# Attention and a cosine MLP in one hand-planned kernel: other landing times for loads and other costs for small operations in its planner, and the first product's scale made per chunk

## The chip, the cores and the metric

The kernel runs on one core of a Trainium2 chip. Its engines are TensorE (PE, matrix products, with its weight loads shown as PEld), VectorE (DVE), ScalarE (ACT), GpSimd (POOL) and SyncE (SP, which issues DMAs). The metric is the time of one execution on the device in microseconds.

## The reference, cut to what matters

The inputs are q, k and v of shape 8 x 8 x 576 x 64 (batch, heads, positions, width), a weight matrix w_in of 512 x 2048 and a matrix w_out of 2048 x 512.

```python
# attention, once on positions averaged in fours, once on a local band
q_d, k_d, v_d = (a.reshape(B, H, S // 4, 4, D).mean(axis=3) for a in (q, k, v))
out_up = np.repeat(sm_attn(q_d, k_d, v_d), 4, axis=2)
mask = np.abs(pos[:, None] - pos[None, :]) < 4
out_local = softmax(where(mask, scale * q @ k.T, -1e9)) @ v
x = (out_up + out_local).transpose(0, 2, 1, 3).reshape(4608, 512)
# the MLP
h = x @ w_in                      # 4608 x 2048
return (h * np.cos(h)) @ w_out    # 4608 x 512
```

## The kernel before, in words

**Two halves.** The attention half works through 8 batches of 4 pairs of heads, 32 units in all. A unit loads q and k (`u_qk`) and a layout of v (`u_v`), forms the scores on PE (`u_s`), transposes (`u_t`) and multiplies with v (`u_pv`), which writes a part of x. `v_sum` adds up v in fours for batches 2 to 7, by one plain load and three DMAs of POOL that add to it.

The MLP half works on tiles of 384 tokens, 12 in all, and on 16 chunks of 128 columns of w_in. `gemm1` makes h for one tile and one chunk (12 products, line 982). `cosine` turns it into g: ACT rounds the scaled h to an integer (L1054), DVE takes the difference (L1055), ACT takes the sine (L1057), DVE multiplies by h and a factor rho (L1058), and the result is stored as two half-precision parts, gh (L1060 on ACT or L1061 on DVE) and gl (L404, on POOL or DVE). `gemm2` multiplies gh and gl by the rows of w_out (9 products, L1079). From tile 5 on, pairs of chunks are made with fewer products (`gemm1_pair`, L1021).

The first three tiles go through blocks of chunks, because the weights arrive during that time: chunk 0, chunk 1, chunks 2 to 4 (2 and 3), then 0 to 4 for the other two tiles, and 4 to 8, 8 to 12 and 12 to 16 for all three. Later tiles take all 16 chunks in one block.

**Weights and scales.** `w_load` loads a chunk of w_in or w_out as 64-bit numbers (512 KB, L427). `w_split` turns them into two half-precision parts: ACT takes an absolute value (L439), DVE does four steps (L440 to L446), ACT squares and sums (L452), PE totals, and DVE reads an exponent (L465). From it small operations make the scale wsc (L468), wexp (L470) and wsum (L471), and with wsc the two parts are made (L477 to L480). For x, `v_norm` loads v once more in four pieces a batch (288 KB each) and squares them on ACT (L499); `x_scale` turns that into a scale for a group of two batches. Three kinds of scale per block follow: `g_scale` gives rho (L562, L564) for a whole block, `h_scale` gives hs, the scale in L1054 and L1055 (L572, L574), and the output's scale os (L577 to L581).

**What sets the order.** Nothing in the kernel is ordered by hand, except PE's MLP products and the chains of loads. Each operation is entered with an engine, a cost in us (`dur`), a time `lat` that must pass after its end before what depends on it may start, and perhaps a second engine as an alternative. `Plan.run` places the operations forward, each on the engine that comes free, by a priority that a backward pass over the same costs has set. Of eight such rounds the shortest is taken, and its order on every engine is the program. At run time each engine issues in that order, and semaphores make it wait for data; an operation whose data is late holds up what stands behind it.

The cost of a load is its size by 262 KB a us, at least 0.45, and it lands `lat` later:

```python
def dma(nbytes, fn, r=(), w=(), pw=()):
    o = pl.op("SP", max(0.45, nbytes / 262e3), fn, r=r, w=w, pw=pw, lat=1.8)
```

The weight loads form a chain in which each waits in the plan for the one before. Loads of `u_qk`, `u_v`, `v_norm` and `v_sum` for batches 2 to 7 may come after the w_out load of chunk 6. The raw weights have 7 buffers, the pieces of v_norm two, the q and k of later units three each, vl two.

A small operation (`small`) is planned on POOL, with DVE as the alternative at 0.08 us. The planner takes the alternative where it would end earlier by a tolerance of 0.3 us.

Of the kernel before, what the change touches and what calls it, by code (L numbers as in the profile page):

```python
# [16 lines left out]
AF = mybir.ActivationFunctionType  # L17
ALU = mybir.AluOpType
# [16 lines left out]
NF = 4  # L35
# [17 lines left out]
ONE = 2.0 ** 23  # L53
# [4 lines left out]
TS = 5  # L58
# [242 lines left out]
def _act(n, psum=True, extra=0):  # L301
    return n * 0.000833 + (0.051 if psum else 0.093) + 0.093 * extra


def _dve(n):
    return n * 0.001042 + 0.065


def _dvs(n):
    return n * 0.001042 + 0.125  # L310
# [7 lines left out]
def attn_ffn_kernel(ctx: ExitStack, tc: tile.TileContext, qT, kT, vdn, vl, w_in, w_out, out):  # L318
    nc = tc.nc
    pe, act, dve, pool, sp = nc.tensor, nc.scalar, nc.vector, nc.gpsimd, nc.sync  # L320
# [6 lines left out]
    pl = Plan()  # L327

    def sb(tag, n, shape, dtype=F32, name=None, pool=None):
        t = pl.turn(tag, n)  # L330
        return pl.buf(lambda: (pool or ap).tile(shape, dtype, name=name or tag, tag=t, bufs=1), t)
# [9 lines left out]
    bquart, bhalf = const.tile([P, 1], F32, name="bquart"), const.tile([P, 1], F32, name="bhalf")  # L341
# [30 lines left out]
    for t in range(NT):  # L372
        r = (t - TS) % (NX - 1)
# [20 lines left out]
    loads, size = {}, {}  # L394

    def dma(nbytes, fn, r=(), w=(), pw=()):
        o = pl.op("SP", max(0.45, nbytes / 262e3), fn, r=r, w=w, pw=pw, lat=1.8)
        size[o] = nbytes if w else 0
        loads.setdefault((pl.name,) + pl.arg, []).append(o)
        return o  # L400

    def sub(n, out, in0, in1, **kw):

        f = lambda e: lambda: e.tensor_tensor(out=out(), in0=in0(), in1=in1(), op=ALU.subtract)  # L404
        pl.op("POOL", _pool(n), f(pool), alts=[("DVE", _dve(n), f(dve))], **kw)

    def small(e, fn, r=(), w=(), pw=()):
        o = {"POOL": ("DVE", 0.08, lambda: fn(dve)), "DVE": None}[e]
        pl.op(e, 0.16 if e == "POOL" else 0.08, lambda: fn({"POOL": pool, "DVE": dve}[e]), r=r, w=w, pw=pw, alts=[o] if o else [])

    def tile1(tag, shape, dtype=F32):
        return pl.buf(lambda: const.tile(shape, dtype, name=tag, tag=tag, bufs=1), tag)
# [17 lines left out]
    exps = {}  # L430
# [53 lines left out]
    xexp = {g: tile1(f"xe{g}", [P, 1]) for g in range(B // GRP)}  # L484
# [1 line left out]
    vq = {g: tile1(f"vq{g}", [P, 8 if g == 0 else 4 * GRP]) for g in range(B // GRP)}  # L486
    vzero = pl.buf(None)
    pl.op("POOL", 0.1, lambda: pool.memset(vq[0].get(), 0.0), w=[vzero])
    hscale, gscale, oscale, passmax = {}, {}, {}, {}

    def later(name, shape):
        n = 2 if name == "vl" else 3
# [73 lines left out]
    def h_scale(g, c0, c1, v):  # L566
        pl.name = "h_scale"
        s, o = (tile1(f"hs{g}{c0}{c1}{v}", [P, c1 - c0], I32), tile1(f"os{g}{c0}{c1}{v}", [P, 1]))
        we, known = (pairexp.get, [paired]) if v else (lambda: wexp.get()[:, 0], [exps[c] for c in range(c0, c1)])
        d, e1, i1 = sb("hd", 2, [P, NC]), sb("oe", 2, [P, 1]), sb("oi", 2, [P, 1], I32)  # L570
        hscale[(g, c0, c1, v)], oscale[(g, c0, c1, v)] = s, o
        small("POOL", lambda e: e.tensor_scalar(out=d.get()[:, :c1 - c0], in0=we()[:, c0:c1], scalar1=xexp[g].get(), scalar2=-29.0,  # L572
                                                op0=ALU.add, op1=ALU.add), r=known + [xexp[g]], w=[d])
        small("POOL", lambda e: e.tensor_scalar(out=s.get(), in0=d.get()[:, :c1 - c0], scalar1=1.0, scalar2=ONE, op0=ALU.max, op1=ALU.mult),  # L574
              r=[d], w=[s])
        pm = passmax[(c0, c1, v)]
        small("POOL", lambda e: e.tensor_scalar(out=e1.get(), in0=pm.get(), scalar1=xexp[g].get(), scalar2=-96.0 if v else -92.0, op0=ALU.add, op1=ALU.add),  # L577
              r=[pm, xexp[g]], w=[e1])
        small("POOL", lambda e: e.tensor_scalar(out=e1.get(), in0=e1.get(), scalar1=1.0, scalar2=254.0, op0=ALU.max, op1=ALU.min), w=[e1])
        small("POOL", lambda e: e.tensor_scalar(out=i1.get(), in0=e1.get(), scalar1=ONE, scalar2=None, op0=ALU.mult), r=[e1], w=[i1])  # L580
        small("POOL", lambda e: e.tensor_scalar(out=o.get(), in0=i1.get().bitcast(F32), scalar1=-2.0 * PI, scalar2=None, op0=ALU.mult),  # L581
              r=[i1], w=[o])
# [45 lines left out]
    def vsum_of(b):  # L628
        if b not in vsum:
            vsum[b] = sb("vsum", 2, [HD, NPAIR, 2, P])  # L630
        return vsum[b]

    def v_sum(b):
        pl.name = "v_sum"
        t = vsum_of(b)
        dst = lambda: t.get().rearrange("p g a n -> p (g a n)")
        src = lambda r: vdn[b][:, r].rearrange("p g a n -> p (g a n)")
        dma(8 * HD * NPAIR * P, lambda: sp.dma_start(dst(), src(0)), w=[t])
        for r in range(1, 4):
            pl.op("POOL", 1.0, lambda r=r: pool.dma_start(dst(), src(r), accum_op=ALU.add), w=[t], lat=6.0)  # L640

    def u_vd(b, pr):
        pl.name = "u_vd"
# [351 lines left out]
    def gemm1_pair(t, p, c0, c1):  # L995
# [45 lines left out]
        add(2, lambda: h1().rearrange("p (i n) -> p i n", i=2), R1, both("ph.1"), [M4, M5], [L1, R1])  # L1041
        cosine(t, 2 * p, c0, c1, h0, [L0, R0])
        cosine(t, 2 * p + 1, c0, c1, h1, [L1, R1])

    def cosine(t, c, c0, c1, h, own):
        m = SIZE[t]
        tr = sb("tr", 4, [P, m], pool=fp)
        gh, gl = sb("gh", LAG + 2, [P, m], F16, pool=fp), sb("gl", LAG + 2, [P, m], F16, pool=fp)
        ti = lambda: tr.get().bitcast(I32)
        g = t // 3  # L1050
        hs, gs = hscale[(g, c0, c1, t >= TS)], gscale[(c0, c1, t >= TS)]
        inv = lambda: hs.get()[:, c - c0:c - c0 + 1].bitcast(F32)
        rho = lambda: gs.get()[:, c - c0:c - c0 + 1].bitcast(F32)
        pl.op("ACT", _act(m, True, 2), lambda: act.activation(ti(), h(), AF.Identity, bias=bquart, scale=inv()), r=own + [hs], w=[tr])  # L1054
        pl.op("DVE", _dvs(m), lambda: dve.scalar_tensor_tensor(out=tr.get(), in0=h(), scalar=inv(), in1=ti(),  # L1055
                                                               op0=ALU.mult, op1=ALU.subtract), r=own + [hs], w=[tr])
        pl.op("ACT", _act(m, False, 1), lambda: act.activation(tr.get(), tr.get(), AF.Sin, scale=2.0 * PI, bias=bhalf), w=[tr], tab="sin")  # L1057
        pl.op("DVE", _dvs(m), lambda: dve.scalar_tensor_tensor(out=tr.get(), in0=tr.get(), scalar=rho(), in1=h(),  # L1058
                                                               op0=ALU.mult, op1=ALU.mult), r=own + [gs], w=[tr])
        pl.op("ACT", _act(m, False), lambda: act.activation(gh.get(), tr.get(), AF.Copy), r=[tr], w=[gh],  # L1060
              alts=[("DVE", _dve(m / 2), lambda: dve.tensor_copy(gh.get(), tr.get()))])  # L1061
        sub(m, gl.get, tr.get, gh.get, r=[tr, gh], w=[gl])
        gt[(t, c)] = (gh, gl)
# [65 lines left out]
    for c in range(NC):  # L1129
        for k, d in (("i", 0.0), ("o", 0.2)):  # L1130
            t = need[c - c % NF] + 0.4 * (c % NF) if c >= NF else need[c]
# [21 lines left out]
    for b in range(2, B):  # L1153
        t0, t1 = tile_of(b * S), tile_of(b * S + S - 1)
        lo, hi = (done[t1 - NX + (t1 >= TS + NX - 1)] if t1 >= NX else 20), first[t0]
        for i in range(NPAIR):

            last = max(lo - 2.5 + (hi - lo - 1.0) * i / (NPAIR - 1), last + 1.5)
            if b % GRP == 0 and i == 0:
                for j in range(GRP):  # L1160
                    at(last - 6.0 + j, v_norm, b + j)
                at(last - 3.5, x_scale, b // GRP)
            if i == 0:
                at(last - 3.0, v_sum, b)
            unit(last, 1.4, 2.5, b, (0, 2, 1, 3)[i])
    for i in range(len(steps) + LAG):
        if i < len(steps):
            t, c, c0, c1 = steps[i]
# [6 lines left out]
    for t, i, f, a in sorted(ev, key=lambda e: e[:2]):  # L1175
        pl.now, pl.arg = t, a
        pl.boost = BOOST.get(a[0], 0.0) if f in (u_qk, u_v, u_vd, u_s, u_t, u_pv, x_scale, v_sum) else 0.0
        if f is u_vd or f is w_split and a[1] == 0 or f is g_scale and a[1] <= NF or f is h_scale and a[2] <= NF:
            pl.boost = BOOST[0]
        f(*a)  # L1180
# [24 lines left out]
    def spare(t0, t1):  # L1205
        best = None
        for own in spans.values():
            for x, y in zip(own, own[1:] + [[1e9]]):
                if x[1] < t1 <= y[0] + 1e-6:
                    if best is None or (max(x[1], t0), x[1]) < best[:2]:  # L1210
                        best = (max(x[1], t0), x[1], x[2])
        return best
# [3 lines left out]
    with tc.manual_schedule():  # L1216
        constants()
        for o in order:
            if o.eng == "PE" and o.start < CFG["fend"]:

                ahead = o.name in ("u_s", "u_t", "u_pv") and o.arg[0] == 0
                s = (last, 0.0, idle) if ahead else spare(last, o.start)
                early = o.name in ("u_s", "u_t", "u_pv") and o.arg[0] < NEARLY
                n = min(int((o.start - s[0] - CFG["fgap"]) / (0.23 if last < 5 else CFG["fstep"])), 16) if s else 0
# [47 lines left out]
```

## Time and profile before

| | |
|---|---|
| median of 3 runs | 995.46 us |
| lowest, highest | 988.75 us, 1001.65 us |
| the profiled execution | 998.38 us, span 996.6 us |
| PE busy | 936.8 us, 94% of the span |
| DVE busy | 808.0 us, 81% |
| ACT busy | 623.4 us, 63% |
| POOL busy | 271.4 us, 27% |
| DMA moved | 84.95 MB, mean 85 GB/s |

The span is the time from the first to the last recorded instruction. Times inside it count from its start. A wait is idle time of an engine put down to what ended it. "DMA to landing" is the time from a DMA's issue until its data is there. The granted clock of TensorE is given as a share of full speed.

### The profile page before, as it was taken

Reading aid. Unit: us, or ns where it says so; the run is one execution under the profiler, and the core shown is the slowest. Engines: PE = TensorE matmul, PEld = TensorE weight load, DVE = VectorE, ACT = ScalarE, POOL = GpSimd, SP = SyncE. Lnnn points to the kernel's source line nnn. Section 1 sums busy time; section 2 is a strip of 40 time slices with the busy share of each in tenths; the row PEclk is TensorE's granted clock in tenths of the full one; section 3 lists DMA queues with packets and bytes.
Section 4 is the critical chain, followed back from the end, with each engine's and each line's share of the span. In section 5 each row is a group of like instructions: output and inputs, shape, how many; then the busy total and the mean of one; then the engine's idle time right before and its main releaser. Section 6 shows DMA issues by size and latency. Waiting matters only on the chain.

```text
span 996.6 us, 28859 instructions
## 1 busy us (share of the span) xinstructions
PE 936.8 (94%) x12163; PEld 612.4 (61%) x12163; DVE 808.0 (81%) x1701; ACT 623.4 (63%) x1342; POOL 271.4 (27%) x401
## 2 busy tenths in 40 slices
PE   5799778989999999999999999999999999999998
PEld 3666334544555555555567666766777677676765
DVE  5889758688897876789997999897779988877775
ACT  2546757887676765656665665765567666655554
POOL 3534744242252230134431143140021311200000
PEclk8989799999999999999999999999999999999999
DMA  8643697873334451140020241140022110000000
GB/s 239 203 169 92 187 241 224 230 197 69 52 82 114 109 117 42 49 113 25 2 73 18 65 123 42 43 120 2 17 74 66 42 50 18 2 33 2 33 1 32
DMA packets 42729, 84.95 MB, mean 85 GB/s; under 512 B 4136, under 2 KB 14632, under 8 KB 42600
## 3 DMA queue, kind: packets, MB, share of 16 engines
q1 hardware_dynamic: 36120, 69.15, 21.6%
q0 software_dynamic: 6480, 13.96, 9.2%
q8 instruction: 95, 1.56, 0.7%
q14 instruction: 34, 0.28, 0.1%
HBM read 65.01 MB, written 18.09 MB: 83 GB/s over the span
## 4 chain that ended last, share of the span: by engine, by line
PE 50%; DVE 21%; ACT 6%; DMA 3%; issue 3%; POOL 1%; POOLq 0%; DVEq 0%; SPq 0%; ACTq 0%
PE bank L1079 22%; PE bank L1021 15%; PE bank L982 6%; DVE tr L1058 3%; DVE tr L1055 3%; PE bank L942 2%; DVE room L1027 2%; PE bank L703 2%; DVE gl L404 2%; DMA k<-kT 2%; DMA norm<-vdn 1%; ACT tr L1054 1%; DVE room L404 1%; PE bank L930 1%; ACT tr L1057 1%
## 5 line engine op out<-in xcount | busy, mean ns | idle before, releaser
L1079 PE MATMUL bank<-wo,gh 128*128 128x512 f16 x1152 | 346.6, 383 | 8.7 <-ACT gh L1060 4.6
L1079 PE MATMUL bank<-wo,gl 128*128 128x512 f16 x576 | 220.3, 383 | 5.7 <-POOL gl L404 3.7
L1079 PEld LDWEIGHTS <-gh 128*128 128x128 f16 x1152 | 109.0, 99 | 100.3 <-issue 11.3
L1057 ACT ACTIVATE tr<-tr,bhalf 128x384 f32<-128x384 f32 x192 | 117.3, 613 | 52.0 <-DVE tr L1055 50.6
L982 PEld LDWEIGHTS <-wi 128*128 128x128 f16 x960 | 94.4, 99 | 84.0 <-issue 18.5
L1027 DVE TENSOR_TENSOR room<-room,bank 128x384 f32<-128x384 f32 x224 | 111.6, 499 | 40.1 <-PE bank L1021 35.9
L1021 PEld LDWEIGHTS <-wi 128*128 128x128 f16 x1344 | 115.5, 98 | 24.8 <-issue 3.9
L1060 ACT ACTIVATE gh<-tr 128x384 f16<-128x384 f32 x167 | 87.1, 523 | 35.7 <-DVE tr L1058 33.8
L404 DVE TENSOR_TENSOR gl<-tr,gh 128x384 f16<-128x384 f32 x159 | 91.5, 577 | 17.9 <-ACT gh L1060 15.5
L1079 PEld LDWEIGHTS <-gl 128*128 128x128 f16 x576 | 56.7, 98 | 78.0 <-POOL gl L404 5.7
L1021 PEld LDWEIGHTS <-room 128*128 128x128 f16 x1008 | 86.4, 98 | 16.9 <-issue 4.8
L1058 DVE SCALAR_TENSOR_TENSOR tr<-tr,rho016True,room 128x384 f32<-128x384 f32 x112 | 71.3, 640 | 12.9 <-ACT tr L1057 12.5
L982 PE MATMUL bank<-x0h,wi 128*128 128x384 f16 x256 | 70.6, 339 | 10.2 <-DVE tr L1058 10.0
L404 POOL TENSOR_TENSOR gl<-tr,gh 128x384 f16<-128x384 f32 x33 | 35.8, 1085 | 156.4 <-ACT gh L1060 103.9
L1054 ACT ACTIVATE tr<-room,bquart,hs3016True 128x384 int32<-128x384 f32 x48 | 33.9, 707 | 53.5 <-DVE room L1027 53.3
L1054 ACT ACTIVATE tr<-room,bquart,hs2016True 128x384 int32<-128x384 f32 x48 | 33.6, 706 | 42.0 <-DVE room L1027 42.0
L942 PEld LDWEIGHTS bank<-sml,vl 32*64 32x64 f32 x3072 | 49.2, 135 | 8.4 <-issue 6.3
L942 PE MATMUL bank<-sml,vl 32*64 32x24 f32 x3072 | 52.6, 214 | 1.5 <-DVE mxl L728 1.1
L760 POOL TENSOR_TENSOR sml<-sml,su 128x384 f32<-128x384 f32 x19 | 21.6, 1134 | 114.5 <-DVE su L758 114.5
L982 PE MATMUL bank<-x0l,wi 128*128 128x384 f16 x128 | 43.3, 339 | 0.0
L1105 POOL DMA_DIRECT2D out<-ob x33 | 30.4, 1075 | 46.8 <-ACT ob L1096 41.0
L703 PE MATMUL bank<-k,q 64*32 64x32 f32 x3072 | 35.7, 196 | 6.8 <-issue 6.4
(312 smaller groups left out, 2117.8 us busy)
## 6 DMA issues: line engine op xcount, KB each, us to landing
vl<-vl SPq DMA_DIRECT2D x32, 384.0 KB, 3.3
q<-qT SPq DMA_DIRECT2D x32, 292.0 KB, 3.6
k<-kT SPq DMA_DIRECT2D x32, 292.0 KB, 4.6
out<-ob SPq DMA_DIRECT2D x36, 256.0 KB, 2.0
out<-ob POOLq DMA_DIRECT2D x33, 256.0 KB, 5.7
wd<-w_in SPq DMA_DIRECT2D x16, 512.0 KB
wd<-w_out SPq DMA_DIRECT2D x16, 512.0 KB, 5.1
norm<-vdn SPq DMA_DIRECT2D x24, 288.0 KB, 5.5
```

Of the source, the lines that this page charges most:

```text
L404: f = lambda e: lambda: e.tensor_tensor(out=out(), in0=in0(), in1=in1(), op=ALU.subtract)
L703: pe.matmul(to()[BS * w:BS * (w + 1), j - c.start], q.get()[hs, o:o + BS], k_.get()[hs, o:o + BS], start=not early, stop=not early or j == ...
L942: pe.matmul(banks[e].get()[64 * h:64 * h + 64, o:o + BQ], vt.get()[r, a, i, :], sml.get()[r, 4 * a + i, :BQ], start=True, stop=True)
L982: pe.matmul(ph.get()[:, :m], w[:, i, kc, :], x[:, kc, :], start=(n == 0), stop=(n == 3 * KC - 1))
L1021: pe.matmul(to.get(), blk(a)[:, kc], x_parts(t)[b][0 if main else 1][:, i, kc], start=(n == 0), stop=(n == 5))
L1027: pl.op("DVE", _dve(n * HT), lambda: dve.tensor_tensor(out=out(), in0=wide(one.get()), in1=two(), op=ALU.add), r=r, w=w)
L1054: pl.op("ACT", _act(m, True, 2), lambda: act.activation(ti(), h(), AF.Identity, bias=bquart, scale=inv()), r=own + [hs], w=[tr])
L1057: pl.op("ACT", _act(m, False, 1), lambda: act.activation(tr.get(), tr.get(), AF.Sin, scale=2.0 * PI, bias=bhalf), w=[tr], tab="sin")
L1058: pl.op("DVE", _dvs(m), lambda: dve.scalar_tensor_tensor(out=tr.get(), in0=tr.get(), scalar=rho(), in1=h(), op0=ALU.mult, op1=ALU.mult), r ...
L1060: pl.op("ACT", _act(m, False), lambda: act.activation(gh.get(), tr.get(), AF.Copy), r=[tr], w=[gh], alts=[("DVE", _dve(m / 2), lambda: dve ...
L1079: pe.matmul(o, (gh, gh, gl)[k].get()[:, sl], wo.get()[:, (0, 1, 0)[k]], start=(c == c0 and k == 0), stop=(c == c1 - 1 and k == 2))
L1105: pl.op("POOL", 1.0, lambda dst=dst, ob=ob: pool.dma_start(dst, ob.get(), accum_op=ALU.add), r=[ob], w=[part[(t, i)]], lat=6.0)
```

## The change

Three numbers of the planner change, and one scale is made in smaller pieces.

- Loads of batches 2 to 7 land later in the plan: `lat` is 6.0 for v_norm, 7.0 for the plain load of v_sum, 5.0 for u_qk and u_v, in place of 1.8. Weight loads of chunks 4 and up have 4.0. The three adding DMAs of v_sum have 9.0 in place of 6.0.
- A small operation costs 0.35 us on POOL in the plan, in place of 0.16. The alternative on DVE stays at 0.08.
- For blocks of at most four chunks (`NF` is 4), `h_scale` makes hs chunk by chunk, two small operations for each, and L1054 and L1055 depend on the piece of their own chunk. Other blocks are made whole, as before.

The arithmetic stays as it is.

```diff
     def dma(nbytes, fn, r=(), w=(), pw=()):
-        o = pl.op("SP", max(0.45, nbytes / 262e3), fn, r=r, w=w, pw=pw, lat=1.8)
+        far = {"v_norm": 6.0, "v_sum": 7.0, "u_qk": 5.0, "u_v": 5.0}.get(pl.name) if pl.arg and pl.arg[0] not in (0, 1) else None
+        if pl.name == "w_load" and pl.arg[1] >= NF:
+            far = 4.0
+        o = pl.op("SP", max(0.45, nbytes / 262e3), fn, r=r, w=w, pw=pw, lat=far or 1.8)
...
     def small(e, fn, r=(), w=(), pw=()):
-        pl.op(e, 0.16 if e == "POOL" else 0.08, ...)
+        pl.op(e, 0.35 if e == "POOL" else 0.08, ...)
...
     def h_scale(g, c0, c1, v):
-        small("POOL", lambda e: e.tensor_scalar(out=d.get()[:, :c1 - c0], in0=we()[:, c0:c1], ...), r=known + [xexp[g]], w=[d])
-        small("POOL", lambda e: e.tensor_scalar(out=s.get(), in0=d.get()[:, :c1 - c0], ...), r=[d], w=[s])
+        n = c1 - c0 if v or c1 - c0 > NF else 1
+        for c in range(c0, c1, n):
+            e_, z, some = pl.buf(None), slice(c - c0, c - c0 + n), known if v else [exps[k] for k in range(c, c + n)]
+            small("POOL", lambda e, c=c, z=z: e.tensor_scalar(out=d.get()[:, z], in0=we()[:, c:c + n], ...), r=some + [xexp[g]], w=[e_], pw=[d])
+            small("POOL", lambda e, z=z: e.tensor_scalar(out=s.get()[:, z], in0=d.get()[:, z], ...),
+                  r=[e_, d], w=[hparts.setdefault((g, c0, c1, v, c), pl.buf(None))], pw=[s])
+            for k in range(c, c + n):
+                hparts[(g, c0, c1, v, k)] = hparts[(g, c0, c1, v, c)]
...
     def v_sum(b):
-            pl.op("POOL", 1.0, lambda r=r: pool.dma_start(dst(), src(r), accum_op=ALU.add), w=[t], lat=6.0)
+            pl.op("POOL", 1.0, lambda r=r: pool.dma_start(dst(), src(r), accum_op=ALU.add), w=[t], lat=9.0)
...
     def cosine(t, c, c0, c1, h, own):
+        hp = hparts[(g, c0, c1, t >= TS, c)]
-        ... act.activation(ti(), h(), AF.Identity, bias=bquart, scale=inv()), r=own + [hs], w=[tr])
+        ... act.activation(ti(), h(), AF.Identity, bias=bquart, scale=inv()), r=own + [hp], w=[tr])
-        ... op0=ALU.mult, op1=ALU.subtract), r=own + [hs], w=[tr])
+        ... op0=ALU.mult, op1=ALU.subtract), r=own + [hp], w=[tr])
```

More of the change, by code (lines that the diff above doesn't have):

```diff
@@ L408, in small @@
         o = {"POOL": ("DVE", 0.08, lambda: fn(dve)), "DVE": None}[e]
-        pl.op(e, 0.16 if e == "POOL" else 0.08, lambda: fn({"POOL": pool, "DVE": dve}[e]), r=r, w=w, pw=pw, alts=[o] if o else [])
+        pl.op(e, 0.35 if e == "POOL" else 0.08, lambda: fn({"POOL": pool, "DVE": dve}[e]), r=r, w=w, pw=pw, alts=[o] if o else [])
     def tile1(tag, shape, dtype=F32):
@@ L488, in attn_ffn_kernel @@
     pl.op("POOL", 0.1, lambda: pool.memset(vq[0].get(), 0.0), w=[vzero])
-    hscale, gscale, oscale, passmax = {}, {}, {}, {}
+    hscale, gscale, oscale, passmax, hparts = {}, {}, {}, {}, {}
     def later(name, shape):
@@ L571, in h_scale @@
         hscale[(g, c0, c1, v)], oscale[(g, c0, c1, v)] = s, o
[L572 to L575, printed above, removed]
+        n = c1 - c0 if v or c1 - c0 > NF else 1
+        for c in range(c0, c1, n):
+            e_, z, some = pl.buf(None), slice(c - c0, c - c0 + n), known if v else [exps[k] for k in range(c, c + n)]
+            small("POOL", lambda e, c=c, z=z: e.tensor_scalar(out=d.get()[:, z], in0=we()[:, c:c + n], scalar1=xexp[g].get(), scalar2=-29.0,
+                                                              op0=ALU.add, op1=ALU.add), r=some + [xexp[g]], w=[e_], pw=[d])
+            small("POOL", lambda e, z=z: e.tensor_scalar(out=s.get()[:, z], in0=d.get()[:, z], scalar1=1.0, scalar2=ONE, op0=ALU.max, op1=ALU.mult),
+                  r=[e_, d], w=[hparts.setdefault((g, c0, c1, v, c), pl.buf(None))], pw=[s])
+            for k in range(c, c + n):
+                hparts[(g, c0, c1, v, k)] = hparts[(g, c0, c1, v, c)]
         pm = passmax[(c0, c1, v)]
@@ L1051, in cosine @@
         hs, gs = hscale[(g, c0, c1, t >= TS)], gscale[(c0, c1, t >= TS)]
+        hp = hparts[(g, c0, c1, t >= TS, c)]
         inv = lambda: hs.get()[:, c - c0:c - c0 + 1].bitcast(F32)
         rho = lambda: gs.get()[:, c - c0:c - c0 + 1].bitcast(F32)
-        pl.op("ACT", _act(m, True, 2), lambda: act.activation(ti(), h(), AF.Identity, bias=bquart, scale=inv()), r=own + [hs], w=[tr])
+        pl.op("ACT", _act(m, True, 2), lambda: act.activation(ti(), h(), AF.Identity, bias=bquart, scale=inv()), r=own + [hp], w=[tr])
         pl.op("DVE", _dvs(m), lambda: dve.scalar_tensor_tensor(out=tr.get(), in0=h(), scalar=inv(), in1=ti(),
-                                                               op0=ALU.mult, op1=ALU.subtract), r=own + [hs], w=[tr])
+                                                               op0=ALU.mult, op1=ALU.subtract), r=own + [hp], w=[tr])
         pl.op("ACT", _act(m, False, 1), lambda: act.activation(tr.get(), tr.get(), AF.Sin, scale=2.0 * PI, bias=bhalf), w=[tr], tab="sin")
```

## The prediction

> **What bounds the kernel now.** I read the page first for the totals, then the table of stretches for where TensorE (PE) is short of work, then the list of waits inside those stretches, and last the timeline around the longest wait.
>
> ```profile
> span 996.6 us, 28859 instructions
> PE 936.8 (94%) x12163; PEld 612.4 (61%) x12163; DVE 808.0 (81%) x1701; ACT 623.4 (63%) x1342; POOL 271.4 (27%) x401
> 0.00:100.00 100.00, 80.45 (x1942) 58.16 (x1943) 80.03 (x209) 48.50 (x147) 40.22 (x65) 0.90 0.58 176
> 100.00:275.00 175.00, 151.47 (x823) 79.74 (x820) 133.26 (x267) 125.98 (x262) 69.35 (x119) 0.94 0.66 170
> 275.00:400.00 125.00, 120.86 (x1961) 71.88 (x1947) 97.11 (x220) 82.86 (x175) 35.45 (x53) 1.00 0.41 93
> 400.00:950.00 550.00, 541.93 (x7143) 374.25 (x7142) 468.19 (x955) 344.26 (x718) 126.43 (x164) 1.00 0.16 46
> ...
> 125.00:150.00 25.00, 18.28 (x93) 9.15 (x91) 13.64 (x28) 13.03 (x26) 10.89 (x16) 0.93 0.93 241
> 200.00:225.00 25.00, 21.41 (x119) 11.48 (x117) 20.38 (x43) 21.10 (x47) 11.30 (x20) 1.00 0.72 198
> ```
>
> The rows of stretches give the stretch and its length, then the busy us (and instructions) of PE, PE's weight load, VectorE (DVE), ScalarE (ACT) and GpSimd (POOL), the granted clock, the busy share of the DMA engines and GB/s. The kernel is bound by PE: 936.8 of 996.6 us. The stretches say where that is not true. From 400 to 950 us PE lacks 550.00 - 541.93 = 8.1 us, so hardly anything can be won there. From 275 to 400 it lacks 4.1 us. From 100 to 275 us, where the weights are loaded and split and the first products run, it lacks 175.00 - 151.47 = 23.5 us, and the granted clock is 0.94. Before 100 us the two first batches run, whose loads keep their 1.8 us; only the small operations change there. So what the change is worth is decided between 100 and 275 us, and at most some 25 to 30 us lie there. The waits of that stretch:
>
> ```profile
> ACT norm L499 <- DMA norm<-vdn: 12.8, 5, 7.7
> DVE wv L440 <- ACT wv L439: 7.5, 1, 7.5
> ACT wi L477 <- POOL wsc L468: 5.0, 4, 2.2
> PE bank L1079 <- ACT gh L1060: 4.6, 1, 4.6
> PE bank L1079 <- POOL gl L404: 3.7, 3, 2.7
> DVE vm L518 <- ACT norm L499: 3.0, 1, 3.0
> ```
>
> Columns: who waited for whom, total us, times, longest. The first, second and fourth are one event, which the timeline shows (start, duration, engine, line, in brackets the wait before it):
>
> ```profile
> 126.69 0.38 SPq L427 DMA_DIRECT2D wd<-w_in  x1
> ...
> 127.12 1.23 SPq L510 DMA_DIRECT2D norm<-vdn  x2
> ...
> 138.54 0.33 PE L982 MATMUL bank<-x2h,wi 128*128 128x384 f16 x1
> 142.26 0.68 ACT L499 ACTIVATE norm<-norm 128x576 f32<-128x576 f32 x1 [7.69 <-DMA norm<-vdn]
> ...
> 143.50 0.67 PE L1079 MATMUL bank<-wo,gh 128*128 128x512 f16 x2 [4.64 <-ACT gh L1060]
> ...
> 144.04 0.68 DVE L440 TENSOR_SCALAR wv<-wv 128x512 f32<-128x512 f32 x1 [7.51 <-ACT wv L439]
> ```
>
> ACT issues in order. At 134.6 it reached the square of a v_norm piece (L499) whose load had left SP at 127 and landed at 142. Behind it stood the rounding gh (L1060), for which PE waited, and the Abs of the next weights (L439), for which DVE waited. The plan had put the square there because it reckoned that load at 288 KB / 262e3 + 1.8 = 2.9 us.
>
> **The change, part by part.** All terms are set against the profiled execution, 998.4 us (span 996.6 and 1.8 around it). It lies 2.9 us above the median of 995.46, inside the spread of 988.75 to 1001.65.
>
> *1. v_norm reckoned at 6.0 + 1.1 us.* What the loads really took from 100 to 175 us, then all weight loads from 100 to 275, then the page's medians:
>
> ```profile
> DMA to landing us min/median/max: 5.0/10.0/15.1
> DMA to landing us min/median/max: 4.1/5.3/7.3
> k<-kT SPq DMA_DIRECT2D x32, 292.0 KB, 4.6
> norm<-vdn SPq DMA_DIRECT2D x24, 288.0 KB, 5.5
> ```
>
> The new figure of 7.1 us is between the median of the busy stretch (10.0) and that of all (5.5); the old one was under the minimum of 5.0. With it the planner finds gh and Abs ready before the square and puts them ahead. The stall goes from ACT for 7.1 - 2.9 = 4.2 of its 7.7 us at least, and with the work put ahead probably all of it goes from PE. PE gets back its 4.6 us of idling, and the slow restart behind it:
>
> ```profile
> 143.40:147.50 4.10, 3.67 (x9) 0.58 0.84 290
> 239.77 1.94 PE bank L1079 x9
> ```
>
> Nine products took about 4.0 us at a granted clock of 0.58, where nine take 1.94 later: 2 us more. So 6.6 us are in reach for PE and 7.5 for DVE. What is late next is DVE, whose row is dense again from 144 us on, fed by the weight loads. Those weights had been issued by 127 us and land within 4.1 to 7.3 us, so they would be there. I take -5, bounds 0 and -7.5. The other four waits on norm, 5.1 us, by stretch, 175 to 200 and 200 to 225 us:
>
> ```profile
> ACT norm L499 <- DMA norm<-vdn: 2.8, 1, 2.8
> ...
> ACT norm L499 <- DMA norm<-vdn: 2.3, 3, 0.9
> ```
>
> From 200 to 225 PE lacks 25.00 - 21.41 = 3.6 us, in which what both waits hold up would have to come back; I take -2, bounds 0 and -3.6.
>
> [...]
>
> *2. u_qk and u_v at 5.0, v_sum at 7.0 and its sums at 9.0.* From 300 to 400 us:
>
> ```profile
> DVE qkd L622 <- DMA k<-kT: 4.5, 3, 2.3
> DVE qkd L622 <- DMA q<-qT: 3.2, 2, 2.1
> ```
>
> 7.7 us of DVE idling, while PE lacks only 4.1 us in that stage and has products queued. I take -1, bounds 0 and -4. POOL waits for vsum, but PE's waits name POOL only at gl, so I cost that at nothing. POOL's slack hides it (69.35 busy of 175). On SP the longer figures raise these loads against the weight loads behind which they queue; SP issues in order, and each norm load first waits for its buffer (two buffers). What this moves is in the bounds of the next term.
>
> *3. w_load of chunks 4 and up at 4.0.* These loads were not waited for:
>
> ```profile
> L439 ACT ACTIVATE wv<-wd 128x512 f32<-128x512 f32 x16 | 10.1, 668 | 0.1
> ```
>
> 0.1 us of idling before 16 of them. So nothing is won. If the plan now holds each split back by 4.0 - 1.8 = 2.2 us and that falls on the end of a block, the three blocks (4 to 8, 8 to 12, 12 to 16) lose 6.6 us together. I take 0, nearest to the row, bounds 0 and +6.6.
>
> *4. Small operations at 0.35 us, and more of them.* Blocks of at most four chunks, all in the first three tiles, are 1+1+2+4+4+4+4 = 20 chunks in 7 blocks, with two operations each. That is 40 instead of 14, so 26 are added. Rows of those there are now:
>
> ```profile
> L562 POOL TENSOR_SCALAR pd12False<-wsum,pm12False 128x1 f32<-128x1 f32 x1 | 5.6, 5582 | 0.1
> L572 POOL TENSOR_SCALAR hd<-wexp,xe 128x4 f32<-128x4 f32 (+3 forms) x7 | 3.5, 493 | 0.7
> L574 POOL TENSOR_SCALAR hs024False<-hd 128x2 int32<-128x2 f32 x1 | 0.9, 935 | 0.1
> L572 DVE TENSOR_SCALAR hd<-wexp,xe x1: 200/200/200, 59.4 to 59.4; 128x1 f32<-128x1 f32 x1
> ...
> 111.34 0.61 PE L1079 MATMUL bank<-wo,gl 128*128 128x512 f16 x1 [2.67 <-POOL gl L404]
> ```
>
> (The first three rows end in busy us, mean ns and idle before; the fourth gives min/median/max ns.) At the 0.49 of seven such operations 26 are 12.8 us of POOL time; on DVE, at 0.2, 5 us. Eight of them (blocks 2 to 4 and 0 to 4) fall near 100 to 110 us, where POOL's chain of scales stood ahead of gl and PE waited 2.7 us for it. Eight at 0.49 make that 3.9 us longer. With 0.35 the planner sees a longer queue and may give gl to DVE, and the 2.7 us go. I take 0, bounds -2.7 and +3.9. Earlier scales themselves win little: Sin may start earlier, but the next product of rho and h still waits for the whole block's rho, which stays as it was, and with it the two banks. So that half is 0.
>
> *5. The rest is planned anew.* From 400 us on the order shifts by itself: 8.1 us lie there to win, and a plan can lose as much as it wins. I take 0, bounds half of that each way, -4 and +4.
>
> The sum: -5 - 2 - 1 + 0 + 0 + 0 = -8, so 990.4 for an execution like the profiled one and **987.5** at the median.
>
> **The rivals.** *The wait only moves* (994): the DMA engines are 0.93 busy from 125 to 150 us, so the norm data come no sooner and each load of them frees its buffer later. The square is then late for x_scale (DVE vm waited 3.0 us for it), and PE waits elsewhere in the same stretch. For it speaks that DVE has 133 us of work in 175; against it that ACT, which stalled, is busy for only 13.03 of the 25 us. That the change does not do what it says, because SP is held by buffers and not by the plan, comes to the same time. [...]
>
> *Slower, by POOL* (1003): POOL's operations are not 0.35 long but as long as DVE lets them. pd12 on one element took 5.58 us while DVE ran its two-input splits; hs024 took 0.94. If the eight added ones near the first block cost that 0.94, they hold wsc and gl back by 7.5 us; all 26 at 0.49 are 12.8 us and give 1008, and with the 6.6 of term 3 1015. It decides from the point where they stand on POOL ahead of wsc or gl. For it: ACT waited 5.0 us for wsc already. Against it: the longer 0.35 sends them to DVE. [...]
>
> *Much faster* (973): all good ends together, 7.5 + 3.6 + 4 + 2.7 + 4 = 21.8 us below 995.46. For it: a stall ahead of the first blocks delays every stage behind it.
>
> **How the numbers follow.** Forecast 0.43; the wait moves, or the change does nothing, 0.18; shorter landing 0.05; slower by POOL 0.19; much faster 0.15. The likeliest gives 987.5. The range 972 to 1008 runs from the good ends together to the 26 operations at 0.49 us; about 0.08 lies below and 0.11 above. A change under 2% (19.9 us) can hardly be told from none here, as three runs spread over 13 us. Faster than 975.6 is nearly all of the much faster case, 0.14; slower than 1015.4 takes a third of the POOL rival with the weights late on top, 0.07; within is 0.79.
>
> **What would show it.** Right: no wait of ACT on norm over 2 us, PE busy over 21 of 25 us from 125 to 150, a clock of 1.0 there, DVE's waits for q and k below 3 us, and the stages after 400 us as long as now. Wrong: PE waiting for wsc or gl at 100 to 112 us longer than 2.7 us, POOL operations over 1 us there, ACT L439 waiting for its loads or standing idle ahead of a block's end, x_scale late. The number fails if the new plan also changes the first 100 us, which I costed at nothing though PE lacks 19.6 us there.

## The result, and the profile after

The changed kernel takes 987.55 us (median of 20 runs, 981.85 to 993.68) where the kernel before takes 996.98 us beside it (20 runs). The ratio is 0.9915, with a 95% interval of 0.9889 to 0.9941: a gain of 0.6 to 1.1%. Some executions of one kernel lie over 1.5% above its fastest; here and below, medians count them and ratios and intervals leave them out. The profiled execution took 986.07 us. First the span and the busy row of the kernel after, from its page:

```profile
span 984.3 us, 28932 instructions
PE 943.4 (96%) x12172; PEld 619.3 (63%) x12172; DVE 813.0 (83%) x1730; ACT 630.3 (64%) x1350; POOL 267.0 (27%) x390
```

The span is 12.3 us shorter, and PE is busy for 6.6 us more, although its work is nearly the same. So the time was won at idle PE, and some of PE's work ran slower. The table of stretches of the kernel after (columns as in the prediction) says where:

```profile
70.00:80.00 10.00, 8.87 (x237) 6.81 (x236) 8.32 (x25) 5.88 (x24) 1.80 (x2) 0.94 0.02 4
80.00:90.00 10.00, 9.73 (x216) 7.54 (x213) 5.78 (x13) 3.64 (x10) 0.00 (x0) 0.50 0.16 56
90.00:100.00 10.00, 9.27 (x53) 5.67 (x53) 6.93 (x17) 5.28 (x14) 1.47 (x4) 0.71 0.25 74
0.00:100.00 100.00, 85.51 (x1892) 60.17 (x1893) 76.06 (x196) 43.97 (x135) 33.41 (x61) 0.76 0.54 165
100.00:275.00 175.00, 162.59 (x981) 89.19 (x980) 150.50 (x315) 136.59 (x283) 86.98 (x137) 0.97 0.69 180
275.00:400.00 125.00, 123.95 (x1992) 74.22 (x1990) 98.16 (x228) 86.48 (x186) 35.35 (x55) 1.00 0.42 93
400.00:950.00 550.00, 541.61 (x7093) 376.45 (x7092) 467.92 (x956) 347.23 (x722) 111.28 (x138) 1.00 0.16 45
125.00:150.00 25.00, 23.01 (x119) 12.13 (x118) 16.95 (x33) 16.62 (x34) 9.19 (x14) 0.93 1.04 301
200.00:225.00 25.00, 22.05 (x123) 12.70 (x122) 24.72 (x52) 20.57 (x45) 17.25 (x24) 0.93 0.77 176
```

From 100 to 275 us PE works 162.59 us and not 151.47, with 981 products and not 823. That is where the gain lies. From 400 to 950 us the row is the old one, 541.61 against 541.93. In the first 100 us something was lost: PE is busy for 5 us more with 50 fewer products, at a granted clock of 0.76 and not 0.90.

All of ScalarE's waits from 100 to 275 us of the kernel after (who waited for whom, total us, times, longest):

```profile
ACT tr L1066 <- DVE tr L1064: 8.1, 12, 1.4
ACT tr L1063 <- PE bank L990: 7.2, 9, 1.5
ACT wd L455 <- DVE wv L449: 6.4, 9, 1.7
ACT gh L1069 <- DVE tr L1067: 5.1, 8, 0.8
ACT wi L480 <- POOL wsc L471: 4.7, 4, 3.3
ACT ob L1105 <- DMA out<-ob: 2.5, 2, 1.5
ACT wv L442 <- DVE wi L483: 2.4, 4, 0.9
ACT ob L1105 <- issue: 0.4, 1, 0.4
ACT wv L442 <- DVE wo L483: 0.2, 1, 0.2
```

ACT no longer waits for norm at all; before, it waited 12.8 us. The squares (L499 before, L502 after) stand later in its order. These rows of the tile norm, before first and after second, end in min/median/max ns and the first and last start:

```profile
L499 ACT ACTIVATE norm<-norm x24: 667/674/697, 106.2 to 221.5; 128x576 f32<-128x576 f32 x24
```

```profile
L502 ACT ACTIVATE norm<-norm x24: 666/670/717, 123.6 to 248.1; 128x576 f32<-128x576 f32 x24
```

The last square begins 26.6 us later, far more than the 4.2 us by which each was planned later. In the timeline of the kernel after, at the place of the old stall, squares and roundings gh (L1069) alternate, and no square has a wait in brackets:

```profile
133.69 0.68 ACT L502 ACTIVATE norm<-norm 128x576 f32<-128x576 f32 x1
...
135.78 0.52 ACT L1069 ACTIVATE gh<-tr 128x384 f16<-128x384 f32 x1 [0.68 <-DVE tr L1067]
...
138.33 0.67 ACT L502 ACTIVATE norm<-norm 128x576 f32<-128x576 f32 x1
```

The next blocks come earlier, as is seen where a block's cosine first uses its scales. Before, then after, blocks 4 to 8 and 8 to 12:

```profile
L1054 ACT ACTIVATE tr<-bank,bquart,hs048False x12: 648/657/677, 169.4 to 215.4; 128x384 int32<-128x384 f32 x12
L1054 ACT ACTIVATE tr<-bank,bquart,hs0812False x12: 654/672/692, 224.5 to 269.0; 128x384 int32<-128x384 f32 x12
```

```profile
L1063 ACT ACTIVATE tr<-bank,bquart,hs048False x12: 652/660/672, 160.1 to 208.2; 128x384 int32<-128x384 f32 x12
L1063 ACT ACTIVATE tr<-bank,bquart,hs0812False x12: 651/657/672, 213.4 to 263.5; 128x384 int32<-128x384 f32 x12
```

Block 4 to 8 comes 9.3 us earlier and block 8 to 12 11.1. For all kernels below one measure of this stage is used, the time from PE's first product of tile 2 (x2h) to its first of tile 3 (x3h), the **weight stage**. For before and after its two ends are the starts in these rows:

```profile
L982 PE MATMUL bank<-x2h,wi x128: 323/326/337, 136.7 to 338.6; 128*128 128x384 f16 x128
L982 PE MATMUL bank<-x3h,wi x128: 323/326/337, 347.8 to 425.9; 128*128 128x384 f16 x128
```

```profile
L990 PE MATMUL bank<-x2h,wi x128: 323/326/336, 139.5 to 329.7; 128*128 128x384 f16 x128
L990 PE MATMUL bank<-x3h,wi x128: 323/326/337, 336.8 to 413.9; 128*128 128x384 f16 x128
```

It went from 211.1 us to 197.3. So 13.8 us were won in it; 2.8 had been lost ahead of it, and tile 3 starts 11.0 us earlier. What follows x3h took 648.8 us before and 647.5 after.

### The profile page after: what moved, and what is told of

Same layout as the page of the kernel before. It is cut to its first block, busy times and chain, and to the rows that moved or that the text cites. A ratio compares the mean times of both kernels' runs of the same rounds, so it can differ in the third digit from the quotient of the medians.

```text
span 984.3 us, 28932 instructions
## 1 busy us (share of the span) xinstructions
PE 943.4 (96%) x12172; PEld 619.3 (63%) x12172; DVE 813.0 (83%) x1730; ACT 630.3 (64%) x1350; POOL 267.0 (27%) x390
## 4 chain that ended last, share of the span: by engine, by line
PE 69%; DVE 17%; POOL 4%; ACT 4%; issue 4%; DMA 1%; POOLq 0%; DVEq 0%; ACTq 0%
PE bank L1088 28%; PE bank L1029 17%; PE bank L990 10%; PE bank L950 4%; PE bank L711 3%; DVE tr L1067 2%; PE bank L1235 2%; DVE room L407 2%; PE bank L938 2%; DVE tr L1064 1%; PE bank L720 1%; PE bank L723 1%; DVE room L1035 1%; DMA out<-ob 1%; ACT tr L1063 1%
## 5 line engine op out<-in xcount | busy, mean ns | idle before, releaser
L1069 ACT ACTIVATE gh<-tr 128x384 f16<-128x384 f32 x166 | 86.3, 521 | 34.6 <-DVE tr L1067 32.7
L407 POOL TENSOR_TENSOR gl<-tr,gh 128x384 f16<-128x384 f32 x35 | 42.8, 1222 | 176.7 <-ACT gh L1069 168.9
L950 PEld LDWEIGHTS bank<-sml,vl 32*64 32x64 f32 x3072 | 53.1, 145 | 7.0 <-issue 5.4
L950 PE MATMUL bank<-sml,vl 32*64 32x24 f32 x3072 | 56.5, 221 | 0.1
L1235 PE MATMUL bank<-ident_b 128*128 128x256 bf16 x188 | 37.9, 327 | 5.8 <-POOL ident_b masks.py:199 3.7
L711 PEld LDWEIGHTS bank<-k,q 64*32 64x32 f32 x3072 | 31.1, 109 | 16.0 <-issue 11.8
```

Of the source, the lines that this page charges most:

```text
L711: pe.matmul(to()[BS * w:BS * (w + 1), j - c.start], q.get()[hs, o:o + BS], k_.get()[hs, o:o + BS], start=not early, stop=not early or j == ...
L950: pe.matmul(banks[e].get()[64 * h:64 * h + 64, o:o + BQ], vt.get()[r, a, i, :], sml.get()[r, 4 * a + i, :BQ], start=True, stop=True)
L1235: pe.matmul(s[2].get()[:, :2 * P], ident_b, ident_b.unsqueeze(1).broadcast_to([P, 2, P]), start=True, stop=True)
```

## The experiments

The expectations set theories against each other by letters. In words: the forecast's own is that one stall of ACT on norm, with its echoes, costs what was won. Against it stand the small operations' new figure, the scale per chunk, and that any new draw of the plan moves the time by this much. One more concerns the lateness at the start. The profiled executions of all kernels by one measure (us; starts from PE's rows of x0h, x2h, x3h; last column the ratio of the timed runs to those of the kernel before beside them, with 95% interval):

| kernel | v_norm at 6.0 | first MLP product (x0h) | weight stage | after x3h | ratio |
|---|---|---|---|---|---|
| before | no | 88.4 | 211.1 | 648.8 | 1 |
| after | yes | 92.4 | 197.3 | 647.5 | 0.9915 [0.9889, 0.9941] |
| e1_move | no, order only | 89.2 | 209.7 | 650.2 | 0.9971 [0.9933, 1.0009] |
| e2_land | yes | 99.5 | 195.8 | 647.4 | 0.988 [0.9832, 0.9928] |
| e3_small | no | 100.1 | 205.9 | 646.7 | 0.9993 [0.9959, 1.0027] |
| e4_chunk | no | 88.9 | 211.3 | 651.1 | 0.9996 [0.9964, 1.0027] |
| e5_null1 | no | 93.6 | 203.0 | 649.1 | 0.9992 [0.9962, 1.0021] |
| e6_null2 | no | 95.2 | 214.2 | 647.1 | 1.0054 [1.0023, 1.0086] |
| e7_norm | yes | 98.1 | 195.2 | 649.0 | 0.9958 [0.9928, 0.9989] |
| e8_wload | no | 89.9 | 202.6 | 650.4 | 0.9992 [0.9951, 1.0033] |
| e9_late | no | 99.6 | 207.6 | 647.5 | 0.9972 [0.9934, 1.0011] |
| e10_land_chunk | yes | 90.3 | 199.1 | 649.6 | 0.9856 [0.9814, 0.9899] |
| e11_land_warm | yes | 100.5 | 196.5 | 650.6 | 0.9918 [0.9886, 0.9949] |
| e12_nonorm | no | 96.9 | 207.0 | 648.9 | 0.9997 [0.996, 1.0034] |

The columns read at a glance: with v_norm at 6.0 the weight stage lies between 195.2 and 199.1, without it between 202.6 and 214.2, and the two groups do not overlap. Nor do they by the start of tile 3 itself, 331.1 to 339.7 us against 342.2 to 353.8, nor by ACT's waits for norm from 100 us on, 0 to 3.6 us in all against 7.8 to 12.8. Inside the second group these waits do not order the stages: e5_null1 waits 9.8 us and has 203.0, e6_null2 waits 8.6 and has 214.2. The kernel before stands near the long end of that group, whose mean is 208.0; the mean of the first group is 196.8. So some 11 of the 13.8 us go with the figure, and some 3 are the luck of the plan of before (an estimate from one execution each). What comes after the stage is the same within 2.3 us of before. The start varies by 10 to 12 us within either group.

**Only the stall taken away (e1_move).** The plan is the old one; in its order alone the squares stand 4.2 us later, with what hangs on them.

```
+ shift = {}
+ for o in order:
+     t = o.start + (4.2 if o.name == "v_norm" and o.eng == "ACT" else 0.0)
+     shift[o] = max([t] + [shift[p] + 1e-6 for p, _ in o.preds])
+ order = sorted(order, key=lambda o: (shift[o], o.start, o.i))
```

> The plan of before, untouched, and only the squares of v_norm come 4.2 us later in the order, with what hangs on them. Theory A (late loads hold ACT, and so DVE and PE): the wait of 7.7 us on norm near 134 us falls under 2 us, PE's 4.6 us idle behind it goes, time 5 to 7 us (0.5 to 0.7%) under before. Theory B (any newly drawn plan differs by as much): nothing is redrawn here, so within 2 us of before, the stall is filled by another wait.

996.2 us, 0.9971 with 1 inside its interval. The stretches of this kernel at the old stall and behind it, then its waits from 100 to 275 us, then a moment of its timeline:

```profile
125.00:150.00 25.00, 22.04 (x123) 11.96 (x122) 19.18 (x41) 18.62 (x40) 11.55 (x15) 1.00 1.05 304
150.00:175.00 25.00, 18.98 (x94) 9.93 (x94) 18.96 (x36) 16.22 (x33) 12.26 (x24) 0.89 0.77 208
```

```profile
PE bank L982 <- DVE tr L1058: 13.5, 5, 4.5
...
ACT norm L499 <- DMA norm<-vdn: 9.1, 7, 2.5
```

```profile
163.95 0.72 ACT L477 ACTIVATE wi<-wv,wsc 128x512 f16<-128x512 f32 x1 [3.50 <-POOL wsc L468]
```

The stall is gone: PE works 22.04 of 25 us where it worked 18.28, at full clock, and no wait on norm is above 2.5. But in the next stretch PE has only 18.98 where it had 21.38, ACT waits there for the next weights' scale, and the weight stage is 1.4 us shorter, not 7. This is what the rival "the wait only moves" described. The interval of the timed runs does not rule out the 5 us of the forecast; the profiled execution shows that its price for this one stall did not come back. The other waits on norm are not settled by it, since 9.1 of 12.8 us of them are left, in smaller pieces.

**Only the landing times (e2_land).** The first hunk of the diff and the 9.0 of the sums.

```
+ far = {'v_norm': 6.0, 'v_sum': 7.0, 'u_qk': 5.0, 'u_v': 5.0}.get(pl.name) if ...
+ if pl.name == "w_load" and pl.arg[1] >= NF:
+     far = 4.0
```

> Only the landing times of the change (all five kinds), small operations at 0.16 and the scale whole per block. Theory A: no wait of ACT on norm over 2 us, and most of the gain of the change, 6 to 10 us under before. Theory B: anywhere within 10 us of before. Theory C (the small operations bring the gain): within 3 us of before.

985.0 us, 0.988: the whole gain. In its stretches PE is as busy from 100 to 275 us as in the kernel after, and the start is as slow:

```profile
0.00:100.00 100.00, 83.13 (x1863) 59.16 (x1864) 66.02 (x179) 42.40 (x134) 28.86 (x53) 0.72 0.51 153
100.00:275.00 175.00, 162.80 (x991) 89.71 (x989) 150.84 (x308) 139.06 (x289) 74.03 (x131) 0.97 0.72 187
```

**Only the small operations at 0.35 (e3_small).**

```
- pl.op(e, 0.16 if e == "POOL" else 0.08, ...
+ pl.op(e, 0.35 if e == "POOL" else 0.08, ...
```

> Only the cost of small operations on POOL, 0.35 in the plan. Theory A: the norm wait stays, time within 3 us of before. Theory B: anywhere within 10 us. Theory C: PE's wait for gl on POOL near 111 us goes and the time is 5 to 9 us under before.

994.48 us, 0.9993. The small operations' figure alone does not bring the gain.

**Only the scale per chunk (e4_chunk).** The hunks of `h_scale` and `cosine`, nothing else.

```
+ n = c1 - c0 if v or c1 - c0 > NF else 1
+ for c in range(c0, c1, n):
...
+ hp = hparts[(g, c0, c1, t >= TS, c)]
```

> Only the scale of the first product made per chunk, costs and landing times as before. Theory A: the norm wait stays, 26 more small operations, 0 to 4 us slower than before. Theory B: anywhere within 10 us. Theory C: as A.

997.28 us, 0.9996. Nor does the scale per chunk. The loss of 7.5 us or more that the rival "slower by POOL" saw in the added operations is ruled out by the interval, which ends at 2.7 us.

**New draws of the plan (e5_null1, e6_null2).** Two constants that say nothing of loads or small operations, nudged until the plan comes out another.

```
- tabpen=3.2
+ tabpen=3.3      # e5_null1
- late=0.17
+ late=0.175      # e6_null2
```

> A control. Only the planner's penalty for changing ACT's table is 3.3 in place of 3.2; no load and no operation is reckoned otherwise. Theory A: within 3 us of before, and a wait on norm of over 4 us is still there. Theory B (any newly drawn plan moves the time as much as the change did): as far from before as the change, 6 us or more either way.

> A second control. Only the planner's delay between two engines is 0.175 in place of 0.17 us. Theory A: within 3 us of before, the wait on norm is still there. Theory B: 6 us or more either way.

993.23 us (0.9992) and 1001.35 us (1.0054). A new draw alone can cost half a per cent, so the luck of the draw is no small matter. The weight stages of the two are 203.0 and 214.2 us, 11 us apart with the loads reckoned alike. But neither of the two gains what the change does, and of the kernels without v_norm's figure none is shown to gain at all.

**Only v_norm at 6.0 (e7_norm).**

```
+ far = {'v_norm': 6.0}.get(pl.name) if pl.arg and pl.arg[0] not in (0, 1) else None
```

> Only v_norm's landing at 6.0. Theory A: no wait of ACT on norm over 2 us and 5 to 7 us under before. Theory B: anywhere within 10 us, with no relation to the waits on norm.

990.19 us, 0.9958. Its stretches:

```profile
0.00:100.00 100.00, 85.30 (x1874) 60.78 (x1875) 70.79 (x191) 43.43 (x135) 38.29 (x64) 0.73 0.53 164
100.00:275.00 175.00, 162.37 (x987) 89.79 (x986) 148.25 (x307) 135.79 (x285) 76.03 (x137) 0.97 0.68 181
```

PE's 162.37 us of work from 100 to 275 are those of the whole change, and the weight stage is the shortest of all, 195.2. Why v_norm's figure alone gives 0.9958 and not the 0.988 of e2_land is not shown. This execution has a clock of 0.73 in the first 100 us, and its first MLP product comes 9.7 us later than before; but e2_land's has 0.72 and comes 11.1 us later. The timed runs speak for the clock all the same: the median of their granted clock is 0.965 here and 0.973 in e2_land (the last section has what that is worth).

**Only w_load at 4.0 (e8_wload), only q, k, v and the sums (e9_late).**

```
+ if pl.name == "w_load" and pl.arg[1] >= NF:
+     far = 4.0                                          # e8_wload
+ far = {'v_sum': 7.0, 'u_qk': 5.0, 'u_v': 5.0}...       # e9_late, with the sums at 9.0
```

> Only the weight loads of chunks 4 and up landing at 4.0. Theory A: these loads were not waited for, so 0 to 6.6 us slower than before, and the norm wait stays. Theory B: anywhere within 10 us.

> Only u_qk, u_v and v_sum landing later (5.0, 5.0, 7.0, and 9.0 for the adding DMAs). Theory A (the time is won by putting v_norm's squares behind the weight splits, 100 to 340 us): DVE's waits for q and k under 2 us, but the squares stay early, the stretch from tile 2's first product to tile 3's stays over 202 us, and the time is 0 to 4 us under before. Rival D (the loads of q, k and v bring half of what all landings bring): 5 to 7 us under before.

996.64 us (0.9992) and 994.41 us (0.9972): no gain is shown for either. By the intervals the first can be worth 5 us at most, the second 7.

**The change without the 0.35 (e10_land_chunk).** It is e2_land and e4_chunk together.

> All landings and the scale per chunk, small operations at 0.16: the change without its cost for small operations. Theory A: as the landings alone, 9 to 13 us under before, a stretch from tile 2 to tile 3 under 199 us. Rival C (the small operations' cost matters): 4 us or more slower than the landings alone.

982.91 us, 0.9856, the fastest of all. Its interval overlaps slightly with that of the whole change (0.9899 against 0.9889), so that it beats the kernel before is shown, and that it beats the change is likely only. Its stretches:

```profile
80.00:90.00 10.00, 9.83 (x340) 7.87 (x336) 10.00 (x24) 6.18 (x17) 2.09 (x2) 1.00 0.01 4
90.00:100.00 10.00, 7.92 (x61) 5.21 (x58) 9.80 (x25) 5.85 (x14) 5.50 (x9) 1.00 0.51 159
100.00:275.00 175.00, 159.88 (x968) 86.17 (x966) 149.07 (x303) 138.66 (x289) 90.86 (x166) 0.99 0.71 179
```

Its weight stage is no shorter than the others'. It has the full clock from 80 to 100 us instead, and starts the MLP at 90.3.

**More warming at the start (e11_land_warm).** The theory is that the late start of e2_land comes from the low clock ahead of 100 us, and that more warming products (products of the identity, whose results nobody uses) would hold it up. Some 20 more of them on top of e2_land, at the second batch's products:

```
- for _ in range(max(n, CFG["warm"][o.arg[0]] if early and s else 0)):
+ for _ in range(max(n, (5 if o.start > 60.0 else CFG["warm"][o.arg[0]]) if early and s else 0)):
```

> The plan with all landings, untouched, and 20 more of the warming products of TensorE ahead of products of batch 1 planned after 60 us (5 ahead of each in place of 1). Theory E (runs of narrow products let TensorE's clock fall to half near 86 us, which makes the first MLP product come at 99 us in place of 88): the clock stays over 0.9 from 80 to 100 us, the first MLP product comes before 95 us, and the time is 3 to 8 us under the landings alone. Its rival (the clock falls for another reason, or the 20 products cost what they save): first product at 98 to 102 us, and within 2 us of the landings alone.

987.73 us, 0.9918, no better than e2_land's 0.988. Its stretches:

```profile
80.00:90.00 10.00, 9.28 (x256) 7.18 (x252) 8.23 (x22) 4.81 (x15) 0.00 (x0) 0.69 0.02 4
90.00:100.00 10.00, 9.94 (x174) 7.28 (x170) 3.57 (x7) 1.96 (x5) 0.00 (x0) 0.63 0.02 3
```

The clock fell at about 84 us, and the added products came between 90 and 99.8. From 90 to 100 us the clock is 0.63, where e2_land has 0.50; the added products may have brought it back, which is not shown, but the first MLP product came no earlier, at 100.5. None of the theory's marks was met, but it is neither confirmed nor refuted, as the products stood behind the fall.

**The whole change but v_norm (e12_nonorm).**

```
- far = {"v_norm": 6.0, "v_sum": 7.0, "u_qk": 5.0, "u_v": 5.0}...
+ far = {"v_sum": 7.0, "u_qk": 5.0, "u_v": 5.0}...
```

> The whole change but for v_norm, which lands after 1.8 as before. Theory A (v_norm's figure is the part that carries the gain): ACT waits for norm over 4 us in all, 9 or more of the 24 squares lie between 170 and 210 us, the stretch from tile 2's first product to tile 3's is over 202 us, and the time is 0 to 4 us under before. Rival D (the other landings carry it too): 6 us or more under before.

995.47 us, 0.9997: the gain is gone. Its wait on norm from 100 to 275 us, the squares, and the stretch:

```profile
ACT norm L502 <- DMA norm<-vdn: 11.2, 6, 5.0
```

```profile
L502 ACT ACTIVATE norm<-norm x24: 665/680/687, 122.5 to 223.4; 128x576 f32<-128x576 f32 x24
```

```profile
100.00:275.00 175.00, 153.10 (x852) 83.36 (x851) 141.74 (x295) 129.96 (x271) 84.18 (x134) 0.99 0.69 179
```

ACT waits for norm again, the last square is back at 223.4, and PE is at 153.10. So the gain needs v_norm's figure, and by e7_norm that figure is enough for the shorter weight stage.

## Why the prediction was right, point by point

The total held: 8 us were forecast, and by the ratio 8.5 of 996.98 came (12.3 between the two profiled executions). That 987.5 was named and 987.55 measured is luck: the three runs it started from had a median 1.5 us lower than the 20 beside the result. Two of its steps were off as well, and their errors partly cancelled.

**Term 1, v_norm's stall: -5, with -2 for the other waits.** The part of the change it named was right: v_norm's figure carries the gain. Size and way were not: the weight stage gave 13.8 us, twice the 7. The step that failed is that each wait was priced by itself, at what PE idled beside it. e1_move removes just the long stall and wins 1.4 us in the stage, while in the five kernels with the new figure the stage is 12 to 16 us shorter than before. What the plan does with the figure is more than a shift by 4.2 us. These are the squares from 170 to 210 us, before first and after second:

```profile
L499 ACT ACTIVATE norm<-norm x12: 667/674/695, 176.3 to 207.9; 128x576 f32<-128x576 f32 x12
```

```profile
L502 ACT ACTIVATE norm<-norm x8: 667/676/682, 172.9 to 206.6; 128x576 f32<-128x576 f32 x8
```

By 210 us ACT has made 20 of the 24 squares in the kernel before, 18 to 22 in the other kernels without the figure, and 14 or 15 in the five with it. In the kernel after, weight splits and cosines stand ahead of them (24 splits begun by 210 us, 22 in the kernel before), and the next blocks come 9 to 11 us earlier. That this room on ACT is what shortens the stage is argued, not shown. Within a group the squares do not order the stages: e8_wload has made 22 by then, the most, and its stage of 202.6 is the shortest without the figure. The figure also moves the norm loads on SP, and no run changed SP's order alone.

**The first 100 us, costed at nothing.** That failed, as the text had named it could. The first MLP product came 4.0 us later, and tile 2 2.8 us later. PE's costliest group of narrow products from 80 to 100 us, before and after (busy us, mean ns):

```profile
L942 PE MATMUL bank<-sml,vl 32*64 32x24 f32 x197 | 3.5, 212 | 0.1
```

```profile
L950 PE MATMUL bank<-sml,vl 32*64 32x24 f32 x196 | 5.9, 277 | 0.1
```

The same work takes 2.4 us longer, at the lower clock (1.00 before, 0.50 after, from 80 to 90 us). The loads of these batches kept their 1.8 us, but the plan before 100 us came out another all the same, as it did in both controls (first MLP product at 93.6 and 95.2 us).

**Term 2, the waits for q and k: -1.** DVE's waits are gone, and POOL has them. From 300 to 400 us of the kernel after:

```profile
POOL qkd L627 <- DMA k<-kT: 20.7, 2, 15.3
```

That is 20.7 us on an engine that is busy for 27% of the span, and PE does not show it: its lack from 275 to 400 us fell from 4.1 to 1.1 us. For these figures alone e9_late has 0.9972 [0.9934, 1.0011], which does not tell 1 us from none.

**Terms 3 and 4: 0.** Each alone agrees with that within its interval, of 3 to 5 us either way: e8_wload gives 0.9992, e3_small 0.9993, e4_chunk 0.9996. POOL's durations were as long as feared and brought no loss that these runs show: one group of the added operations in the kernel after,

```profile
L578 POOL TENSOR_SCALAR hd<-wexp,xe 128x1 f32<-128x1 f32 (+1 forms) x21 | 11.0, 523 | 1.9
```

has a mean of 0.52 us, more than the 0.49 that the forecast's rival reckoned with. That DVE sets their length, as that rival has it, is not shown in general. In the kernel before pd12 took 5.58 us with DVE at work beside it throughout, and pd812, the same operation on four columns, 0.32 us at 224.5 us with DVE idle; but pd24 took 0.33 us at 103.4 us with DVE at work on L1058 beside it. Beside the rest of the change the 0.35 may cost some us (e10_land_chunk), which is not shown.

**Term 5, the rest planned anew: 0, within 4.** It held for what follows tile 3's start, where no kernel is over 2.3 us from before. Ahead of it a new draw does more than 4 us, by the table's start column and by e6_null2's 1.0054.

**The rivals.** "The wait only moves" is what e1_move does, not the change. The chance of 0.05 for a shorter landing is that loads land sooner than the new figures say and what uses them is held back for nothing; no run shows that loss. In the kernel before, the norm loads landed after 5.0 us at the least and 10.0 at the median from 100 to 175 us, where its plan had 2.9. In e7_norm the landings that its trace gives are 3.2 to 4.2 us, under the 7.1 planned, and it is at 0.9958 all the same; e2_land, with 3.0 to 12.5, is at 0.988. Of the marks set beforehand, no wait on norm, PE at 23.01 of 25 us, DVE's waits and the stages from 400 us on were met; the clock from 125 to 150 us is 0.93 still, not 1.0. Of the marks of a wrong forecast one was approached: between 100 and 112 us PE waited 2.2 us for weights that ACT could not make before their wsc, under the mark of 2.7.

## What to carry to other kernels

Give a planner the landing times that loads have in the busy stretch where they are waited for; here the gain hung on one landing figure out of six. Do not price a stall by what idles beside it: take it away alone and see whether another wait takes its place, and look at what the whole new order does with the stage. And where a plan is drawn by search, time a few changes that should do nothing, since they set the size from which a gain is more than luck, here about half a per cent.

## What the runs showed of the hardware that was not expected

TensorE's clock fell to half while the engine was recorded busy. In the kernel after it is 0.50 from 80 to 90 us with 9.73 of 10 us busy, and 8.87 in the ten before. The kernel before, in the same places of its span:

```profile
80.00:90.00 10.00, 9.94 (x256) 7.58 (x252) 9.06 (x22) 5.93 (x17) 0.50 (x1) 1.00 0.24 71
90.00:100.00 10.00, 8.12 (x65) 5.97 (x63) 9.83 (x23) 6.01 (x14) 9.20 (x11) 1.00 0.56 168
```

It has full clock at the same busy share. PE is hardly idle around the fall: from 70 to 90 us of the kernel after all its idle times together are 1.4 us. The cause is open. The mix of products differs a little there: before had 24 warming products of 128 rows in those 20 us and after 15, among narrow products of 32 rows. That runs of narrow products let the clock fall is an argument, and the traces do not settle it. In the kernel after two runs of 96 narrow products (32x24) start at 74.9 and 77.9 us, and the clock falls at 79; in the kernel before two such runs start at 74.7 and 78.1 us, with three warming products between them and not two, and the clock stays at 1.00. In e10_land_chunk 340 products run from 80 to 90 us, against 216 in the kernel after, and the clock is 1.00 too. e11_land_warm put its products too late to test it.

This clock also goes with most of the spread between runs. Over the 104 timed runs of the kernel before that list it, the span falls by 7.2 us for each 0.01 of mean granted clock (0.958 to 0.983, correlation -0.84); within each other kernel it is 5 to 10 us. The median clock is 0.974 for before and 0.971 for after. By that slope, an estimate, this is 2 us of loss, against the 4.0 by which the first MLP product comes later in the two profiled executions. So the start column of the table, one execution each, is rougher than the column of the weight stage. By the same estimate the clock is worth what e6_null2 lost and much of what e7_norm lacks: their medians are 0.966 and 0.965, that of before beside them 0.975, which is 6 to 7 us.
